# Attention and a maxout network: a pair's rows as seven units, one load each for queries and keys, four loads for values

## The chip, the cores and the metric

The kernel runs on one core of one Trainium2 chip. A core has five engines that run side by side and meet through semaphores: TensorE (PE in the profile; its weight loads are PEld), VectorE (DVE), ScalarE (ACT), GpSimd (POOL) and SyncE (SP), which here does nothing but issue DMA transfers. Transfers run on the core's 16 DMA engines. The metric is the device time of one execution in microseconds; lower is better.

## What is computed

Attention with normed queries and keys, for 8 images (batch entries) and 12 heads of 448 tokens and 64 channels; its output, with the heads side by side as 768 channels, goes through a layer with three weight matrices of which the elementwise largest is kept, and a second layer.

```python
batch, n_heads, seq, head_dim = (8, 12, 448, 64)
n_tokens, d_model, d_ff = (3584, 768, 768)

def rmsnorm(x, g):
    rms = np.sqrt(np.mean(x * x, axis=-1, keepdims=True) + 1e-06)
    return x / rms * g
q_n, k_n = (rmsnorm(q, g_q), rmsnorm(k, g_k))
scores = scale * np.matmul(q_n, k_n.transpose(0, 1, 3, 2))
scores = scores - np.max(scores, axis=-1, keepdims=True)
attn = np.exp(scores)
attn = attn / (np.sum(attn, axis=-1, keepdims=True) + 1e-09)
return np.matmul(attn, v).astype(np.float32)
...
h = np.maximum(np.maximum(x @ w1, x @ w2), x @ w3)
return (h @ w_out).astype(np.float32)
```

All inputs and the output are 32-bit floats.

## The kernel before

**Pairs and units.** The work is cut into 48 pairs of heads (G = 48, six pairs an image, g counts them). A pair has 2 x 448 = 896 rows of queries, of keys and of values, which is seven units of 128 rows: units 0 to 2 are rows of the first head, unit 3 holds the last 64 rows of the first head in the lower 64 partitions and the first 64 of the second head in the upper ones, and units 4 to 6 are rows of the second head. A tile of rows is 128 partitions x 7 units x 64 channels.

**Two ways.** The first six pairs (PLAIN = 6, the first image) are computed in 32-bit floats and turned on PE, because the weights of the network aren't ready yet. From pair 6 on each 32-bit operand is split in two 16-bit parts, a high and a low one, and the products of the parts are added up. Turning (rows to columns) is then done by DMA transposes: keys and queries in line 450 (`turn_rows`), the softmax weights pp into pt in lines 735 and 741 (`turn_weights`, five transposes a pair).

**The exchanged copy of the keys.** The turned keys kt hold the high parts in one half of the partitions and the low parts in the other. `swap_keys` (line 457) makes a second copy with the halves exchanged by two transfers from SBUF to SBUF, and the scores (line 584) are the sum of a matmul with each copy. The first scores of a pair are issued in the last beat of the pair before. `swap_values` (line 558) does the like for the values.

**Loads of rows.** `load_rows` loads queries or keys by four transfers a pair: three units of each head (96 KB, line 342) and 64 rows of each head (16 KB, line 344). Keys are read three neighbouring rows to a partition (runs of 768 bytes in memory), queries one row to a partition (256 bytes). `load_v` loads values by seven transfers (lines 360 to 370) into a tile of four units for each head, so that some rows lie in it twice; most of its rows are read in threes, too. The row order of keys and values is the same, and so doesn't change the result. As three keys of one partition follow each other, the low parts of the softmax weights are written in reversed blocks of 64 (`lower_weights`, line 719), and the values' exchanged copy is met in reversed order. All of these transfers are issued by SyncE, except two of the first pair's keys, which ScalarE issues.

**Order of the work.** The order on every engine is that of the program, written out by hand: `beat(g, i)` with 12 beats a pair. A quarter of a pair (c = i // 3) goes through scores, the row's largest (line 606), exponentials (line 622), division and high part (line 708), low part (line 719) and transposes. Meanwhile `thirds` feeds PE with matmuls of the network for the image before (lines 796 and 856). `later(n, work)` puts work n beats later. SyncE's queue gets in a pair: loads of keys (beat 0) and queries (beat 1) three pairs ahead, the last transposes of weights of the pair before (beat 2), the exchanged values (beat 3), the transposes of keys and queries of the next pair (beats 4 and 5), in beat 5 the values six pairs ahead and the first transpose of weights, in beat 8 the exchanged keys and the second transpose of weights, in beat 11 the third; stores of results and loads of network weights come between. It takes them strictly in this order, and a step that waits holds all that stand behind it.

**Values' largest.** `largest_v` lets DVE look for the largest value of a pair once its values are there, four beats after the load in a pair later on (three in the first pair, which loads the values of seven pairs, one in each of beats 0 to 6); `bound_v` combines six pairs of an image by a small matmul.

**Buffers.** kr and qr have two buffers each, vr seven, pp three, kt, qt and pt two, vs two.

Of the kernel before, what the change touches and what calls it, by code (L numbers as in the profile page):

```python
# [11 lines left out]
F16 = mybir.dt.float16  # L12
AF = mybir.ActivationFunctionType
ALU = mybir.AluOpType
AX = mybir.AxisListType.X

P = 128
# [16 lines left out]


PLAIN = 6


@with_exitstack
def qknorm_attention_maxout_ffn_kernel(  # L40
# [35 lines left out]
    nc = tc.nc  # L76
    B, H, S, D = q.shape
# [35 lines left out]
    def later(beats, work, last=False):  # L113

        due.setdefault(clock[0] + beats, ([], []))[last].append(work)
# [203 lines left out]

    st = {}  # L320

    def at_unit(g, h, c):

        if g < PLAIN:
            return 2 * c + h
        return 4 * h + c

    def rest(g):
        return 6 if g < PLAIN else 3

    def load_rows(g, name, src, on):
        b, pr = divmod(g, NP)
        t = sb.tile([P, UNITS, D], F32, name=name, bufs=2)
        for h, half in enumerate(HALVES):
            rows = src[b, 2 * pr + h]
            first = LEFT * h
            if name == "kr":
                main = rows[first:first + 3 * P].rearrange("(p c) d -> p c d", c=3)
            else:
                main = rows[first:first + 3 * P].rearrange("(c p) d -> p c d", p=P)  # L340
            units = slice(h, 6, 2) if g < PLAIN else slice(4 * h, 4 * h + 3)
            on[h].dma_start(out=t[:, units], in_=main)
            last = rows[0:LEFT] if h else rows[3 * P:S]
            on[h].dma_start(out=t[half, rest(g)], in_=last)
        st.setdefault(g, {})[name] = t

    def load_q(g):
        load_rows(g, "qr", q, (nc.sync, nc.sync))

    def load_k(g):  # L350
        load_rows(g, "kr", k, (nc.sync, nc.sync if g else nc.scalar))


    def load_v(g):
        b, pr = divmod(g, NP)
        t = sb.tile([P, 2, 4, D], F32, name="vr", bufs=7)
        lower, upper = HALVES
        on = nc.sync
        rows = v[b, 2 * pr]
        on.dma_start(  # L360
            out=t[:, 0, 0:3], in_=rows[0:3 * P].rearrange("(p c) d -> p c d", c=3)
        )
        for half in HALVES:
            on.dma_start(out=t[half, 0, 3], in_=rows[3 * P:S])  # L364
        rows = v[b, 2 * pr + 1]
        main = rows[LEFT:S].rearrange("(p c) d -> p c d", c=3)
        on.dma_start(out=t[lower, 1, 0], in_=rows[0:LEFT])
        on.dma_start(out=t[upper, 1, 0:3], in_=main[lower])  # L368
        on.dma_start(out=t[lower, 1, 1:4], in_=main[upper])
        on.dma_start(out=t[upper, 1, 3], in_=main[upper, 2])  # L370
        st.setdefault(g, {})["vr"] = t


# [176 lines left out]
            op=ALU.subtract,  # L550
        )

    def swap_values(g):

        s = st[g]
        s["vs"] = sb.tile([P, 8, D], F16, name="vs", bufs=2)
        for to, of in (HALVES, HALVES[::-1]):
            nc.sync.dma_start(out=s["vs"][to], in_=s["vp"][of, 0])


    SHIFT = (LEFT, 0)
# [135 lines left out]
    def upper_weights(g, c):  # L697
        s = st[g]
        sc, n = s["sc", c], banks(c)
        rs = sb.tile([P, 2], F32, name="rs", bufs=3)  # L700
        nc.vector.tensor_scalar(  # L701
            out=rs[:, :n], in0=sc[:, 1, S + 8:S + 8 + n], scalar1=SUM_EPS,
            scalar2=1.0 / P_UP, op0=ALU.add, op1=ALU.mult,
        )
        nc.vector.reciprocal(rs[:, :n], rs[:, :n])
        pp = sb.tile([P, 2, 2 * S], F16, name="pp", bufs=3)
        for h in range(n):
            nc.scalar.activation(  # L708
                pp[:, h, :S], sc[:, h, :S], AF.Copy, scale=rs[:, h:h + 1]
            )  # L710
        s["pp", c] = pp
        s["rs", c] = rs

    def lower_weights(g, c):

        s = st[g]
        sc, rs, pp = s.pop(("sc", c)), s.pop(("rs", c)), s["pp", c]
        for h in range(banks(c)):
            nc.vector.scalar_tensor_tensor(  # L719
                out=pp[:, h, S:].rearrange("p (u k) -> p u k", k=LEFT)[:, ::-1],  # L720
                in0=sc[:, h, :S].rearrange("p (u k) -> p u k", k=LEFT),
                scalar=rs[:, h:h + 1],
                in1=pp[:, h, :S].rearrange("p (u k) -> p u k", k=LEFT),
                op0=ALU.mult, op1=ALU.subtract,
            )

    def turn_weights(g, c):
        s = st[g]
        pp = s.pop(("pp", c))
        if c == 0:  # L730
            s["pt"] = sb.tile([P, 14, 512], F16, name="pt", bufs=2)
        pt = s["pt"]
        if c < 3:
            first = LEFT + c * P
            nc.sync.dma_start_transpose(  # L735
                out=pt[:, :, first:first + P], in_=pp.rearrange("p h k -> p (h k)")
            )
            return
        for h, half in enumerate(HALVES):
            first = 0 if h else LEFT + 3 * P  # L740
            nc.sync.dma_start_transpose(
                out=pt[:, 7 * h:7 * h + 7, first:first + LEFT], in_=pp[half, 0]
            )


# [1 line left out]
    def add_values(g):  # L747
        s = st[g]
        av = ps_a.tile([P, 512], F32, name="av", tag="a")
        s["av"] = av  # L750
        if g < PLAIN:
            vr, pt = s["vr"], pt_plain(s)
            for u in range(4):
                rows = HALVES[0] if u == 3 else slice(0, P)
                for h, half in enumerate(HALVES):
                    nc.tensor.matmul(
                        av[half, :S], vr[rows, h, u], pt[rows, h, u],
                        start=u == 0, stop=u == 3,
                    )
            return  # L760
        vp, vs, pt = s["vp"], s["vs"], s["pt"]
        steps = [(part, u, u) for u in range(4) for part in range(2)]
        steps += [(2, 2 - i, 4 + i) for i in range(3)]
        for n, (part, u, block) in enumerate(steps):
            for h, half in enumerate(HALVES):
                values = vs[:, 4 * h + u] if part == 2 else vp[:, part, 4 * h + u]
                nc.tensor.matmul(  # L767
                    av[half, :S], values, pt[:, 7 * h + block, SHIFT[h]:SHIFT[h] + S],
                    start=n == 0, stop=n == len(steps) - 1,
                )  # L770
# [228 lines left out]
    def beat(g, i):  # L999
# [44 lines left out]
        if g + 1 < G:  # L1044
# [5 lines left out]
            else:  # L1050
# [3 lines left out]
                    lower_rows(g + 1, "kq"[i - 2])  # L1054
                if i in (4, 5):
                    turn_rows(g + 1, "kq"[i - 4])
                if i == 8:
                    swap_keys(g + 1)

        if n < G:  # L1060
# [9 lines left out]
        if g == 0 and i < 7:  # L1070
            load_v(i)
            later(3, lambda: largest_v(i))
        if 0 < g < G - 6 and i == 5:
            load_v(g + 6)
            later(4, lambda: largest_v(g + 6))
        if g == 0 and i == 9:
            bound_v(0)
        if g > 1 and g % NP == 0 and g < G and i == 1:
# [5 lines left out]
        if PLAIN <= w and i == 0:  # L1084
            lower_v(w)
        if PLAIN <= w and i == 3:
            swap_values(w)

        if g + 3 < G:
            if i == 0:  # L1090
# [54 lines left out]
```

## Time and profile before

| | |
|---|---|
| median of 3 runs | 1278.85 us (1277.87 to 1281.59) |
| the profiled execution: its time | 1279.71 us |
| its span, from first to last instruction | 1277.6 us |
| PE busy | 1054.4 us (83%) |
| DVE busy | 712.9 us (56%) |
| ACT busy | 640.1 us (50%) |
| POOL busy | 615.5 us (48%) |
| mean clock granted to PE | 0.915 of full speed |
| DMA packets of the queue that SyncE feeds | 480736, 166.12 MB, 63.5% of 16 engines' span |

Times in the profile are microseconds, unless marked ns. A group of instructions is shown as line, engine and operation, tile written and tile read, shapes, count; then its busy time in all, the mean of one in ns, and the idle time of the engine just ahead of it with what ended most of that. The timeline shows start, duration and what ran; rows of SPq are SyncE's queue issuing transfers, and their duration is that of issuing, not of the transfer. "Issue to landing" is the transfer's own time. Releasers are inferred from semaphores.

### The profile page before, as it was taken

The page shows a single profiled execution, that of the slowest core. Times are in us where ns is not written, and L with a number is a line of the kernel's source. Part 1 is how long each engine was busy: PE and PEld are TensorE (multiplying, and loading weights), DVE is VectorE, ACT ScalarE, POOL GpSimd, SP SyncE. Part 2 cuts the span into 40 slices and gives each one's busy share as a digit, 9 for nine tenths or more (in the row PEclk, how much of TensorE's full clock was granted, in tenths as well). Part 3 has the DMA queues.
Part 4 walks back from the last instruction along what each step waited for, and adds up shares of the span by engine and source line. Part 5 has one row for each costly group of instructions (what it writes and reads, how often), then busy time and mean ns, then how long its engine had stood idle before and what let it go on. Part 6 is the DMA issues. An engine that isn't in the chain of part 4 may idle for free. (4 is left out here: it accounts for less than half of the span.)

```text
span 1277.6 us, 18009 instructions
## 1 busy us (share of the span) xinstructions
PE 1054.4 (83%) x5850; PEld 545.4 (43%) x5850; DVE 712.9 (56%) x1348; ACT 640.1 (50%) x1437; POOL 615.5 (48%) x661
## 2 busy tenths in 40 slices
PE   5398688779688886887888788788878879999998
PEld 3254344334243443443444344344434435455555
DVE  3499879676455644565455554555545555565110
ACT  3278777456445454553545455354544546564111
POOL 4257968545454553554455455455535545551000
PEclk9598879899798998899889898988988999999999
DMA  4455578777767667776767767676676669885001
GB/s 123 108 155 161 158 166 162 144 132 145 146 124 145 122 134 162 138 129 124 158 132 123 144 137 155 126 142 122 132 155 131 127 128 173 157 142 109 26 1 50
DMA packets 481757, 167.63 MB, mean 131 GB/s; under 512 B 429568, under 2 KB 477440, under 8 KB 481664
## 3 DMA queue, kind: packets, MB, share of 16 engines
q1 hardware_dynamic: 480736, 166.12, 63.5%
q8 instruction: 46, 0.75, 0.3%
q10 hardware_dynamic: 928, 0.38, 0.1%
q14 instruction: 47, 0.39, 0.1%
HBM read 53.54 MB, written 11.01 MB: 51 GB/s over the span
## 5 line engine op out<-in xcount | busy, mean ns | idle before, releaser
L796 PE MATMUL acc<-xt,w_sb 128*128 128x448 f16 x2592 | 550.4, 371 | 0.0
L796 PEld LDWEIGHTS <-w_sb 128*128 128x128 f16 x2592 | 263.3, 103 | 273.8 <-issue 65.2
L622 ACT ACTIVATE sc<-sc,nm 128x448 f32<-128x448 f32 x294 | 178.8, 608 | 238.8 <-DVE nm L606 234.1
L708 ACT ACTIVATE pp<-sc,rs 128x448 f16<-128x448 f32 x294 | 173.0, 634 | 227.8 <-DMA pt<-pp 183.9
L606 DVE TENSOR_REDUCE nm<-sc 128x2 f32<-128x896 f32 x192 | 186.7, 973 | 165.9 <-PE sc L584 94.5
L584 PE MATMUL sc<-kt,qt 128*128 128x448 f16 x504 | 136.8, 386 | 164.9 <-DMA kt<-kt 158.3
L719 DVE SCALAR_TENSOR_TENSOR pp<-sc,rs,pp 128x448 f16<-128x448 f32 x294 | 188.0, 676 | 1.7 <-ACT pp L708 1.7
L856 PE MATMUL acc<-wo_sb,ht 128*128 128x384 f16 x864 | 154.9, 336 | 0.0
L402 POOL TENSOR_TENSOR ri<-ri,half_neg 128x7 f32<-128x7 f32 x96 | 146.4, 1525 | 8.0
L825 POOL COPY hx<-ht 128x128 f16<-128x128 f16 x48 | 15.6, 325 | 271.5 <-DVE ht L820 271.5
L584 PEld LDWEIGHTS <-qt 128*128 128x128 f16 x504 | 48.2, 102 | 222.4 <-DMA kt<-kt 172.7
L548 POOL TENSOR_TENSOR vp<-vr,vp 128x512 f16<-128x512 f32 x42 | 49.2, 1172 | 168.8 <-ACT vp L542 168.8
L856 PEld LDWEIGHTS <-ht 128*128 128x128 f16 x864 | 86.1, 101 | 65.2 <-issue 13.7
L165 DVE TENSOR_REDUCE v_rows<-vr 128x1 f32<-128x512 f32 x48 | 32.8, 684 | 114.9 <-DMA vr<-in_v_dram 114.9
L782 DVE SCALAR_TENSOR_TENSOR xt<-av,xt 128x448 f16<-128x448 f32 x42 | 26.2, 624 | 91.8 <-ACT xt L781 91.7
L767 PE MATMUL av<-pt,vp 128*64 128x448 f16 x672 | 74.0, 360 | 3.5 <-DMA qr<-in_q_dram 1.8
L436 POOL TENSOR_TENSOR kp<-kn,kp 128x448 f16<-128x448 f32 x42 | 45.6, 1085 | 60.9 <-ACT kp L430 60.7
L388 DVE TENSOR_REDUCE ss<-sq 128x7 f32<-128x448 f32 x96 | 57.7, 602 | 13.1 <-ACT sq L379 10.0
L436 POOL TENSOR_TENSOR qp<-qn,qp 128x448 f16<-128x448 f32 x42 | 43.5, 1036 | 26.6 <-ACT qp L430 23.4
L701 DVE TENSOR_SCALAR rs<-sc 128x2 f32<-128x2 f32 (+1 forms) x168 | 26.3, 157 | 52.3 <-ACT sc L622 52.3
L810 DVE TENSOR_TENSOR m<-acc,m 128x448 f32<-128x448 f32 x48 | 29.7, 618 | 42.7 <-PE acc L796 39.4
L767 PEld LDWEIGHTS <-vp 128*64 128x64 f16 x672 | 35.8, 111 | 38.7 <-issue 15.1
(126 smaller groups left out, 1236.7 us busy)
## 6 DMA issues: line engine op xcount, KB each, us to landing
raw<-in_moe_w_dram SPq DMA_DIRECT2D x18, 768.0 KB, 4.5
kt<-kt SPq DMA_DIRECT2D x84, 112.0 KB, 2.9
qr<-in_q_dram SPq DMA_DIRECT2D x96, 96.0 KB, 2.3
out_dram<-osb SPq DMA_DIRECT2D x24, 384.0 KB, 2.8
kr<-in_k_dram SPq DMA_DIRECT2D x95, 96.0 KB, 2.9
vs<-vp SPq DMA_DIRECT2D x84, 64.0 KB, 2.0
vr<-in_v_dram SPq DMA_DIRECT2D x48, 96.0 KB, 2.5
vr<-in_v_dram SPq DMA_DIRECT2D x96, 48.0 KB, 2.2
```

The lines of the kernel that those rows point to most:

```text
L388: nc.vector.tensor_reduce(sums[g % 2][:, KQ[what]], sq, axis=AX, op=ALU.add)
L402: nc.gpsimd.tensor_tensor(out=ri, in0=ri, in1=half_neg[:, at], op=ALU.pow)
L436: nc.gpsimd.tensor_tensor(out=parts[:, :, 1], in0=n, in1=parts[:, :, 0], op=ALU.subtract)
L548: nc.gpsimd.tensor_tensor(out=vp[:, 1], in0=vr.rearrange("p h n d -> p (h n) d"), in1=vp[:, 0], op=ALU.subtract,)
L584: nc.tensor.matmul(sc[:, h, :S], qt[:, 4 * h + c], kt[:, n, keys[h]], start=n == 0, stop=n == 1,)
L606: nc.vector.tensor_reduce(nm[:, :n], sc[:, :n, :S], axis=AX, op=ALU.max, negate=True)
L622: nc.scalar.activation(to, sc[:, h, :S], AF.Exp, bias=nm[:, h:h + 1], accum_out=total,)
L708: nc.scalar.activation(pp[:, h, :S], sc[:, h, :S], AF.Copy, scale=rs[:, h:h + 1])
L719: nc.vector.scalar_tensor_tensor(out=pp[:, h, S:].rearrange("p (u k) -> p u k", k=LEFT)[:, ::-1], in0=sc[:, h, :S].rearrange("p (u k) -> p ...
L767: nc.tensor.matmul(av[half, :S], values, pt[:, 7 * h + block, SHIFT[h]:SHIFT[h] + S], start=n == 0, stop=n == len(steps) - 1,)
L796: nc.tensor.matmul(acc[:, :S], wt[:, wp, c], xs[c][:, xp], start=(c == 0 and n == 0), stop=(c == NCT - 1 and n == 2),)
L856: nc.tensor.matmul(acc[:, :HW], lhs, wo_sb[:, f, wp, half * HW:(half + 1) * HW], start=(f == 0 and n == 0), stop=(f == NFT - 1 and n == 2),)
```

## The change

Tiles of queries, keys and values are all read one row to a partition, in order. Queries and keys of a split pair come in one load of seven units (224 KB) each; for the six plain pairs in three. Values come in four loads: three units of each head, and two for the fourth units of both heads. The names LOADS and the choice of ScalarE as issuer are new: a pair from number 48 on would be loaded by ScalarE, and the pairs are 0 to 47. The low parts of the softmax weights keep their order, and the exchanged copy of the values becomes a shifted copy of three units a head instead of four (`shift_values`, 48 KB instead of 64 KB a transfer). The exchange of the keys is issued in beat 7 instead of 8, the load of values in beat 6 instead of 5, with DVE's search three beats after it instead of four.

```diff
 PLAIN = 6
+LOADS = 48
...
     def load_rows(g, name, src, on):
+
         b, pr = divmod(g, NP)
         t = sb.tile([P, UNITS, D], F32, name=name, bufs=2)
-        for h, half in enumerate(HALVES):
-            rows = src[b, 2 * pr + h]
-            first = LEFT * h
-            if name == "kr":
-                main = rows[first:first + 3 * P].rearrange("(p c) d -> p c d", c=3)
-            else:
-                main = rows[first:first + 3 * P].rearrange("(c p) d -> p c d", p=P)
-            units = slice(h, 6, 2) if g < PLAIN else slice(4 * h, 4 * h + 3)
-            on[h].dma_start(out=t[:, units], in_=main)
-            last = rows[0:LEFT] if h else rows[3 * P:S]
-            on[h].dma_start(out=t[half, rest(g)], in_=last)
+        rows = src[b, 2 * pr:2 * pr + 2].rearrange("h s d -> (h s) d")
+        rows = rows.rearrange("(n p) d -> p n d", p=P)
+        if g < PLAIN:
+            for h in range(2):
+                on[h].dma_start(out=t[:, h:6:2], in_=rows[:, 4 * h:4 * h + 3])
+            on[1].dma_start(out=t[:, 6], in_=rows[:, 3])
+        else:
+            on[0].dma_start(out=t, in_=rows)
         st.setdefault(g, {})[name] = t
 
     def load_q(g):
-        load_rows(g, "qr", q, (nc.sync, nc.sync))
+        load_rows(g, "qr", q, (nc.sync, nc.sync) if g < LOADS else (nc.scalar,))
 
     def load_k(g):
-        load_rows(g, "kr", k, (nc.sync, nc.sync if g else nc.scalar))
+        first = (nc.sync, nc.sync if g else nc.scalar)
+        load_rows(g, "kr", k, first if g < LOADS else (nc.scalar,))
...
         t = sb.tile([P, 2, 4, D], F32, name="vr", bufs=7)
-        lower, upper = HALVES
-        on = nc.sync
-        rows = v[b, 2 * pr]
-        on.dma_start(
-            out=t[:, 0, 0:3], in_=rows[0:3 * P].rearrange("(p c) d -> p c d", c=3)
-        )
-        for half in HALVES:
-            on.dma_start(out=t[half, 0, 3], in_=rows[3 * P:S])
-        rows = v[b, 2 * pr + 1]
-        main = rows[LEFT:S].rearrange("(p c) d -> p c d", c=3)
-        on.dma_start(out=t[lower, 1, 0], in_=rows[0:LEFT])
-        on.dma_start(out=t[upper, 1, 0:3], in_=main[lower])
-        on.dma_start(out=t[lower, 1, 1:4], in_=main[upper])
-        on.dma_start(out=t[upper, 1, 3], in_=main[upper, 2])
+        rows = v[b, 2 * pr:2 * pr + 2]
+        for h in range(2):
+            nc.sync.dma_start(
+                out=t[:, h, 0:3], in_=rows[h, 0:3 * P].rearrange("(u p) d -> p u d", p=P)
+            )
+        for half, part in zip(HALVES, (rows[:, 3 * P:S], rows[:, 0:LEFT])):
+            nc.sync.dma_start(out=t[half, :, 3], in_=part.rearrange("h p d -> p h d"))
...
-    def swap_values(g):
+    def shift_values(g):
...
-        s["vs"] = sb.tile([P, 8, D], F16, name="vs", bufs=2)
-        for to, of in (HALVES, HALVES[::-1]):
-            nc.sync.dma_start(out=s["vs"][to], in_=s["vp"][of, 0])
+        t = s["vs"] = sb.tile([P, 2, 3, D], F16, name="vs", bufs=2)
+        vp = s["vp"][:, 0].rearrange("p (h n) d -> p h n d", h=2)
+        lower, upper = HALVES
+        nc.sync.dma_start(out=t[lower], in_=vp[upper, :, 0:3])
+        nc.sync.dma_start(out=t[upper], in_=vp[lower, :, 1:4])
...
     def lower_weights(g, c):
...
-                out=pp[:, h, S:].rearrange("p (u k) -> p u k", k=LEFT)[:, ::-1],
-                in0=sc[:, h, :S].rearrange("p (u k) -> p u k", k=LEFT),
-                scalar=rs[:, h:h + 1],
-                in1=pp[:, h, :S].rearrange("p (u k) -> p u k", k=LEFT),
-                op0=ALU.mult, op1=ALU.subtract,
+                out=pp[:, h, 1], in0=sc[:, h, :S], scalar=rs[:, h:h + 1],
+                in1=pp[:, h, 0], op0=ALU.mult, op1=ALU.subtract,
...
     def add_values(g):
...
-        steps += [(2, 2 - i, 4 + i) for i in range(3)]
+        steps += [(2, u, 4 + u) for u in range(3)]
...
-                values = vs[:, 4 * h + u] if part == 2 else vp[:, part, 4 * h + u]
+                values = vs[:, h, u] if part == 2 else vp[:, part, 4 * h + u]
...
     def beat(g, i):
...
-                if i == 8:
+                if i == 7:
                     swap_keys(g + 1)
...
-        if 0 < g < G - 6 and i == 5:
+        if 0 < g < G - 6 and i == 6:
             load_v(g + 6)
-            later(4, lambda: largest_v(g + 6))
+            later(3, lambda: largest_v(g + 6))
...
         if PLAIN <= w and i == 3:
-            swap_values(w)
+            shift_values(w)
```

More of the change, by code (lines that the diff above doesn't have):

```diff
@@ L320, in qknorm_attention_maxout_ffn_kernel @@
     st = {}
[L322 to L329, printed above, removed]
     def load_rows(g, name, src, on):
@@ L705, in upper_weights @@
         nc.vector.reciprocal(rs[:, :n], rs[:, :n])
-        pp = sb.tile([P, 2, 2 * S], F16, name="pp", bufs=3)
+        pp = sb.tile([P, 2, 2, S], F16, name="pp", bufs=3)
         for h in range(n):
             nc.scalar.activation(
-                pp[:, h, :S], sc[:, h, :S], AF.Copy, scale=rs[:, h:h + 1]
+                pp[:, h, 0], sc[:, h, :S], AF.Copy, scale=rs[:, h:h + 1]
             )
@@ L735, in turn_weights @@
             nc.sync.dma_start_transpose(
-                out=pt[:, :, first:first + P], in_=pp.rearrange("p h k -> p (h k)")
+                out=pt[:, :, first:first + P], in_=pp.rearrange("p h a k -> p (h a k)")
             )
@@ L741, in turn_weights @@
             nc.sync.dma_start_transpose(
-                out=pt[:, 7 * h:7 * h + 7, first:first + LEFT], in_=pp[half, 0]
+                out=pt[:, 7 * h:7 * h + 7, first:first + LEFT],
+                in_=pp[half, 0].rearrange("p a k -> p (a k)"),
             )
```

## The prediction

> **What bounds the kernel now.** I read the page's costliest groups first, because PE is the busiest engine. The matmuls of the scores carry nearly all of its waiting, and one transfer ends it, the exchanged copy of the turned keys (issued in line 457):
>
> ```profile
> span 1277.6 us, 18009 instructions
> ...
> L584 PE MATMUL sc<-kt,qt 128*128 128x448 f16 x504 | 136.8, 386 | 164.9 <-DMA kt<-kt 158.3
> ...
> kt<-kt SPq DMA_DIRECT2D x84, 112.0 KB, 2.9
> ```
>
> The last column of the second row says that PE stood 164.9 us ahead of these matmuls, 158.3 of it for that copy. The third row (the page's DMA issues) says that one copy needs 2.9 us from issue to landing, so it is not slow: it is issued late. So the next view is the timeline of SyncE's queue (start, duration, line), here one whole pair of heads, from one exchange to the next:
>
> ```profile
> 1026.20 1.77 SPq L457 DMA_DIRECT2D kt<-kt  x2
> 1028.09 3.82 SPq L735 DMA_TRANSPOSE pt<-pp  x2
> 1032.03 0.98 SPq L342 DMA_DIRECT2D kr<-in_k_dram  x1
> 1033.06 0.51 SPq L344 DMA_DIRECT2D kr<-in_k_dram  x1
> ...
> 1037.24 0.67 SPq L344 DMA_DIRECT2D qr<-in_q_dram  x1
> 1038.02 2.53 SPq L741 DMA_TRANSPOSE pt<-pp  x2
> 1040.66 1.17 SPq L558 DMA_DIRECT2D vs<-vp  x2
> 1041.93 1.24 SPq L450 DMA_TRANSPOSE kt<-kp  x1
> 1043.27 1.24 SPq L450 DMA_TRANSPOSE qt<-qp  x1
> 1044.57 0.57 SPq L360 DMA_DIRECT2D vr<-in_v_dram  x1
> ...
> 1048.30 0.59 SPq L370 DMA_DIRECT2D vr<-in_v_dram  x1
> 1048.99 1.55 SPq L735 DMA_TRANSPOSE pt<-pp  x1
> 1050.59 1.77 SPq L457 DMA_DIRECT2D kt<-kt  x2
> ```
>
> Each row starts within about 0.1 us of the end of the one before. SyncE issues without pause, 24.39 us a pair (1050.59 - 1026.20), and nothing else in the kernel needs that long. **SyncE's issuing is the bound.** The same view where no loads are left, two and three pairs from the end:
>
> ```profile
> 1113.07 1.90 SPq L457 DMA_DIRECT2D kt<-kt  x2
> 1115.09 3.82 SPq L735 DMA_TRANSPOSE pt<-pp  x2
> 1120.29 2.67 SPq L741 DMA_TRANSPOSE pt<-pp  x2
> 1123.08 2.25 SPq L558 DMA_DIRECT2D vs<-vp  x2
> 1125.43 1.24 SPq L450 DMA_TRANSPOSE kt<-kp  x1
> 1126.77 1.25 SPq L450 DMA_TRANSPOSE qt<-qp  x1
> 1128.11 1.62 SPq L735 DMA_TRANSPOSE pt<-pp  x1
> 1129.83 1.72 SPq L457 DMA_DIRECT2D kt<-kt  x2
> 1131.65 3.62 SPq L735 DMA_TRANSPOSE pt<-pp  x2
> 1138.51 2.50 SPq L741 DMA_TRANSPOSE pt<-pp  x2
> ```
>
> Now SyncE has gaps, and the chain that ended last runs through PE alone there:
>
> ```profile
> 1112.93 0.38 PE sc L591 x4
> ...
> 1131.51 0.38 PE sc L591 x4
> ...
> 1135.97 0.76 PE sc L584 x4
> ...
> 1150.09 0.38 PE sc L591 x4
> ```
>
> Equal points of three pairs are 18.58 us apart (1131.51 - 1112.93, 1150.09 - 1131.51). That is PE's own pair, with softmax and splitting at their full pace beside it. So the trace holds a sample of the kernel with SyncE unburdened: 18.58 against 24.39.
>
> The last view sets both stretches side by side (window and length; busy time of PE, its loads, DVE, ACT, POOL with counts; granted clock; DMA share; GB/s):
>
> ```profile
> 1028.09:1052.47 24.38, 20.21 (x116) 10.43 (x116) 14.17 (x29) 11.92 (x28) 13.61 (x16) 0.93 0.67 131
> 1115.09:1131.65 16.56, 16.56 (x102) 8.53 (x99) 11.83 (x25) 11.34 (x26) 9.71 (x12) 1.00 0.79 148
> ```
>
> DVE, ACT and POOL need at most 14.2 us a pair, so none of them is next. The 16 DMA engines are busy 0.67 x 24.38 = 16.3 us a pair with loads and 0.79 x 16.56 = 13.1 without: the loads cost them about 3.2 us.
>
> **The change part by part.** Where do the sums apply? The first exchange of the even stretch is quoted below; the one at 1113.07 is 38 pairs later, 933.52 us, so 24.57 a pair with the stores of results that some pairs carry (24.39 without). After 1113.07 come 164.5 us that hold no loads of rows and only work that the change leaves as it is.
>
> ```profile
> 179.55 1.13 SPq L457 DMA_DIRECT2D kt<-kt  x2
> ```
>
> *Queries and keys.* Eight issues a pair become two. The eight take 5.99 us (1032.03 to 1038.02). What does a load of 896 pieces cost to issue? No row shows one. The nearest is a weight block, 768 KB in 768 pieces:
>
> ```profile
> 10.41 1.17 SPq L218 DMA_DIRECT2D raw<-in_moe_w_dram  x2
> 11.72 0.58 SPq L342 DMA_DIRECT2D kr<-in_k_dram  x1
> ```
>
> Two of these take 1.17 and the load behind them 0.58, like any other, so issue does not grow with the pieces: 0.55 each, the lower end. The upper end is 1.24, the row of a transpose that reads a tile of the same 128 x 7 units. I take 0.55, as it is a plain load. The first behind the transposes keeps its 0.98. So 0.98 + 0.55 and two gaps of 0.05 make 1.63: 4.36 saved. Eight rows that nothing stretched (0.98 and seven of about 0.6 with gaps) would take 5.1, and 3.5 would be saved. The upper end gives back up to 1.4.
>
> *Values.* Seven issues take 4.42 us (1044.57 to 1048.99), 0.63 each with gaps; four take 2.53: 1.89 saved. Together 5.4 to 6.25 a pair leave SyncE 18.3 to 19.2 of the 24.57; I take 18.8. SyncE was the issuer of these loads before, too (the branch for ScalarE needs a pair 48, and the last is 47), so that part of the change moves nothing.
>
> *Exchange in beat 7, values in beat 6.* The load of values goes behind the first transpose of weights, the exchange stays behind both. What is issued between the transposes of keys and queries and the exchange is then 1.62 + 2.53 in place of 4.42 + 1.55: only the 1.9 that is counted already. The beat itself matters once SyncE has slack. Does the copy then come in time? Put the four loads into the quoted pair without loads, behind 1128.11: the exchange ends at 1129.83 + 1.72 + 2.53 = 1134.1; its second half, issued some 0.85 sooner, lands 2.9 later, at 1136.1. PE wants it at 1135.97. That is 0.2 late; with the usual 1.17 for vs in place of 2.25 it is 0.9 early. DVE's search for the largest value stays in its beat (one later, one less of delay), and its wait for the loads shrinks with them.
>
> *Where SyncE's next turn falls.* In the same pair the transposes from 1131.65 now end at 1137.8, the two loads at 1139.4, and the next step is due at 1138.51: 0.9 late, or 0.2 early with vs at 1.17. Stores come on top: three an image and two more every second image, so 27 in the seven images of these 38 pairs; at 0.6, an issue like any other, 0.4 a pair. So SyncE (18.8) and PE (18.58) are nearly even and hand each other a wait now and then. I take **19.0 us a pair**, 0.2 over the larger.
>
> *Splitting and shifted copy.* DVE's low parts lose their reversed blocks; DVE is hidden (14.17 of 24.38), and if it became bound this could only help: 0. The shifted values are 48 KB a copy in place of 64, still two issues: 0. The matmuls are as many.
>
> *More and smaller pieces.* Keys were 384 pieces a pair, queries 896, values 512; now 896, 896 and 1024. So 1792 become 2816 for nearly the same bytes. The engines' 3.2 us stay 3.2 (by bytes) or become 5.0 (by pieces); with 13.1 and about 1.1 for stores (some 245 KB a pair, at the rate of the loads' 752 KB in 3.2) that is 17.4 to 19.2 a pair. By the upper end it would equal my pair; I keep it as a bound. The Trainium skill speaks against this part: "DMA: Bandwidth & Descriptors", section "Why small descriptors are slow (HBM only)", gives a 256-byte piece 11 cycles for 8 of data. By that a 768-byte run cut in three costs 33 cycles for 27, and the estimate for the loads would be at most 3.9 us, inside my ends. No run here shows a piece's price by itself.
>
> *Start.* The first beats load seven pairs' values, and PE waits for the largest value of the first six:
>
> ```profile
> 48.74 0.48 SPq L370 DMA_DIRECT2D vr<-in_v_dram  x1
> ...
> 52.80 0.56 PE L517 MATMUL most<-v_most,ones_c 128*128 128x1 f32 x2 [13.67 <-DVE v_most L510]
> ...
> 160.13 1.30 PE L584 MATMUL sc<-kt,qt 128*128 128x448 f16 x3 [6.73 <-DMA kt<-kt]
> ```
>
> The first row is the last load of the sixth pair. Ahead of it 18 issues of values go (0.64 each with gaps, 11.5) and 8 of keys and queries (0.6, 4.8): some 16 us sooner. The 13.67 us wait of the second row goes, with what other chains keep: I take 13, between 8 and 17. At the first split pair (third row) seven loads become four ahead of the exchange: 3 of the 6.73.
>
> *Sum.* 179.55 - 13 - 3 = 163.5; 38 x 19.0 = 722; 164.5 for the end; 2.1 around the span (the profiled execution took 1279.71 us for a span of 1277.6). 163.5 + 722 + 164.5 + 2.1 = **1052 us**. The profiled execution is 0.9 above the median of 1278.85, which changes nothing.
>
> **The rivals.**
>
> *PE alone is the bound.* SyncE's savings hold at their larger end and its waits fit into its slack: 18.1 to 18.58 a pair (some pairs hold a little less work of the network than the quoted ones), 1018 to 1036 us. For it: the pairs without loads. Against it: stores, and the exchange that is just in time.
>
> *Transfers or dearer issue give part of it back.* At 1.24 for a large load the pair is 20.4; if the loads' service doubled to 6.4, the engines need 13.1 + 6.4 + 1.1 = 20.6, with transposes blocking SyncE meanwhile: 330.1 + 38 x 20.5 = 1109 us. For it: 17.4 to 19.2 of 19.0 leaves the engines little air, and two transposes in a row take 3.82 (1028.09) where one takes 1.55, so the queue holds SyncE up already. Against it: the share is 0.67 now. The skill's same page, in "Specifications", gives 512 B as the least size for full rate, which points this way.
>
> *Slower than before.* The place is the DMA queue from loads to transposes: if small pieces hold the engines for more than 24.57 - 13.1 - 1.1 = 10.4 us a pair, transposes land too late and the pair grows beyond today's. That is 10.4 x 16 / 2816 = 59 ns for a piece on one engine, against 3.2 x 16 / 1792 = 29 ns now, where half of the pieces already have 256 B. At 65 ns the pair is 25.6: 330.1 + 973 = 1303 us.
>
> *It does not do what it says.* The issue time saved comes back whole as longer transposes, because the queue behind SyncE was the limit: 1263 us, the 16 at the start aside. Against it: DMA at 0.67, and load rows of even 0.5 to 0.6 us.
>
> **How the numbers follow.** Forecast, 18.6 to 19.6 a pair (1037 to 1075 us): 0.52. PE alone: 0.20. Part given back (1075 to 1170): 0.24. Nothing gained: 0.02. Slower: 0.02. The range leaves out about one in ten on each side: 1020 to 1112, which takes in both ends of the issue price and of the start. A measurement of this kernel tells 0.3% (4 us) from no change: faster 0.97, same 0.01, slower 0.02.
>
> **What would show it.** PE's wait for kt falls from 158 to under 30 us; exchanges stand 18.6 to 19.6 us apart; two rows of about 0.55 to 1.0 for keys and queries and four of 0.6 for values; PE's granted clock near 1.00 in the pairs, DMA share about 0.9 (17.4 of 19.0); no wait of 13 us near 40. Wrong if large loads take over 1.2 us to issue, if the transposes behind them grow by more than a microsecond, or if another wait (weights for pt, values for DVE) takes the place of kt.

## The result and the profile after

The changed kernel takes 1091.12 us (median of 4 runs, 1090.79 to 1095.35); the kernel before took 1278.36 us beside it. The ratio is 0.854, 95% interval 0.8513 to 0.8566. The forecast was 1052 us and the range 1020 to 1112. The profiled execution took 1095.35 us, the longest of the four, with a span of 1093.6.

The page of the changed kernel, with the rows that answer to those of before (busy times; the scores' matmuls with PE's wait ahead of them; the exchanged copy and its time to land):

```profile
PE 996.9 (91%) x5850; PEld 526.8 (48%) x5850; DVE 705.5 (65%) x1348; ACT 637.6 (58%) x1437; POOL 615.2 (56%) x661
...
L573 PE MATMUL sc<-kt,qt 128*128 128x448 f16 x504 | 123.6, 360 | 54.6 <-DMA kt<-kt 41.7
...
kt<-kt SPq DMA_DIRECT2D x84, 112.0 KB, 2.3
```

PE's wait for the exchanged keys fell from 158.3 to 41.7 us. The same matmuls also became cheaper, 360 ns in place of 386. That is the granted clock, as the windows by stage show, first of the kernel before, then of the changed one. The two stages are the first nine pairs after the exchange of pair 7 and the 29 behind them (the cut in the first fence is some 7 us off the exchange of pair 16). The columns are window and length, busy time of PE, its loads, DVE, ACT and POOL with counts, granted clock, DMA share, GB/s:

```profile
179.55:400.00 220.45, 176.79 (x954) 87.76 (x954) 146.63 (x280) 124.83 (x274) 125.07 (x130) 0.89 0.74 145
400.00:1113.07 713.07, 596.30 (x3322) 299.99 (x3320) 386.12 (x778) 353.89 (x823) 365.29 (x412) 0.92 0.71 139
```

```profile
164.32:357.22 192.90, 171.94 (x994) 86.39 (x995) 146.94 (x284) 126.44 (x278) 130.35 (x135) 0.96 0.86 169
357.22:927.82 570.60, 542.59 (x3269) 282.50 (x3269) 379.94 (x772) 348.95 (x814) 357.19 (x404) 1.00 0.90 170
```

Over both stages PE was idle for 160.4 us before (933.5 - 773.1) and 49.0 after (763.5 - 714.5), and its busy time fell by 58.6 us for nearly the same matmuls. The granted clock accounts for that fall: its mean over both stages is 0.913 before and 0.990 after, and 773.1 x 0.913 / 0.990 = 713, against 714.5 measured. So of the 170 us that these 38 pairs lost, 111 were waiting and 59 were slower clock. The rest of the gain is the start: the exchange of pair 7 came at 179.55 and comes at 164.32. The wait of 13.67 us for the values' largest stands at 6.87 now:

```profile
39.71 0.56 PE L504 MATMUL most<-v_most,ones_c 128*128 128x1 f32 x2 [6.87 <-DVE v_most L497]
```

What follows the exchange of pair 45 takes 165.8 us, as before (164.5).

These exchanges in SyncE's timeline, of pairs 7, 16 and 45, give the pace:

```profile
164.32 1.14 SPq L444 DMA_DIRECT2D kt<-kt  x2
...
357.22 1.19 SPq L444 DMA_DIRECT2D kt<-kt  x2
...
927.82 1.71 SPq L444 DMA_DIRECT2D kt<-kt  x2
```

That is 20.09 us a pair over all 38, against 24.57 before and 19.0 in the forecast: 21.43 in the first nine and 19.68 in the other 29.

One later pair in SyncE's queue, in the same form as the pair that the prediction shows:

```profile
834.25 1.15 SPq L444 DMA_DIRECT2D kt<-kt  x2
835.51 4.87 SPq L720 DMA_TRANSPOSE pt<-pp  x2
840.47 1.00 SPq L336 DMA_DIRECT2D kr<-in_k_dram  x1
841.58 0.56 SPq L336 DMA_DIRECT2D qr<-in_q_dram  x1
842.24 2.50 SPq L726 DMA_TRANSPOSE pt<-pp  x2
844.83 0.65 SPq L546 DMA_DIRECT2D vs<-vp  x1
845.54 0.62 SPq L547 DMA_DIRECT2D vs<-vp  x1
846.26 1.25 SPq L437 DMA_TRANSPOSE kt<-kp  x1
847.61 1.24 SPq L437 DMA_TRANSPOSE qt<-qp  x1
848.94 1.58 SPq L720 DMA_TRANSPOSE pt<-pp  x1
850.58 1.70 SPq L353 DMA_DIRECT2D vr<-in_v_dram  x2
852.32 1.32 SPq L357 DMA_DIRECT2D vr<-in_v_dram  x2
853.74 1.19 SPq L444 DMA_DIRECT2D kt<-kt  x2
```

There are still hardly any gaps: 19.49 us of nearly pure issuing. SyncE is the bound of the later pairs after the change, too (e4 and e9 below test it). Adding up all rows of its queue between the exchanges of pairs 16 and 41, 25 pairs that have all loads, gives these means (us a pair; each group is the sum of its rows' durations, "between" the sum of the pauses from one row to the next):

```
                        before  after  e6     e3     e5     e4     e9
loads of keys, queries   4.79   1.46   5.02   1.48   1.33   -      -
loads of values          4.38   3.00   4.66   2.63   2.97   3.11   -
transposes of weights    8.12   8.61   8.19   8.40   8.33   8.40   9.41
transposes of keys, q.   2.61   2.60   2.59   2.54   2.54   2.57   2.56
exchange of keys         1.64   1.22   1.66   1.67   1.23   1.23   1.40
copy of values           1.22   1.37   1.30   1.28   1.32   1.32   1.29
stores                   0.43   0.42   0.40   0.47   0.41   0.53   0.42
between                  1.58   1.18   1.16   1.16   1.25   1.93   3.52
pair                    24.78  19.86  24.99  19.64  19.40  19.09  18.60
```

(e6, e3, e5, e4 and e9 are experiments below.)

### The profile page after: what moved, and what is told of

It is laid out like the page before. It is cut to its first block, busy times and chain, and to the rows that moved or that the text cites. A ratio compares the mean times of both kernels' runs of the same rounds, so it can differ in the third digit from the quotient of the medians.

```text
span 1093.6 us, 17471 instructions
## 1 busy us (share of the span) xinstructions
PE 996.9 (91%) x5850; PEld 526.8 (48%) x5850; DVE 705.5 (65%) x1348; ACT 637.6 (58%) x1437; POOL 615.2 (56%) x661
## 3 DMA queue, kind: packets, MB, share of 16 engines
q1 hardware_dynamic: 525600, 164.70, 75.4%
## 5 line engine op out<-in xcount | busy, mean ns | idle before, releaser
L782 PE MATMUL acc<-xt,w_sb 128*128 128x448 f16 x2592 | 517.3, 355 | 0.0
L782 PEld LDWEIGHTS <-w_sb 128*128 128x128 f16 x2592 | 252.7, 98 | 245.9 <-issue 18.0
L573 PE MATMUL sc<-kt,qt 128*128 128x448 f16 x504 | 123.6, 360 | 54.6 <-DMA kt<-kt 41.7
L842 PE MATMUL acc<-wo_sb,ht 128*128 128x384 f16 x864 | 148.5, 326 | 0.7 <-DVE ht L806 0.5
L842 PEld LDWEIGHTS <-ht 128*128 128x128 f16 x864 | 83.2, 98 | 61.1 <-issue 4.7
L753 PE MATMUL av<-pt,vp 128*64 128x448 f16 x672 | 71.6, 356 | 0.0
L753 PEld LDWEIGHTS <-vp 128*64 128x64 f16 x672 | 34.5, 109 | 34.1 <-issue 12.5
```

The costliest lines, as they stand in the source:

```text
L573: nc.tensor.matmul(sc[:, h, :S], qt[:, 4 * h + c], kt[:, n, keys[h]], start=n == 0, stop=n == 1,)
L753: nc.tensor.matmul(av[half, :S], values, pt[:, 7 * h + block, SHIFT[h]:SHIFT[h] + S], start=n == 0, stop=n == len(steps) - 1,)
L782: nc.tensor.matmul(acc[:, :S], wt[:, wp, c], xs[c][:, xp], start=(c == 0 and n == 0), stop=(c == NCT - 1 and n == 2),)
L842: nc.tensor.matmul(acc[:, :HW], lhs, wo_sb[:, f, wp, half * HW:(half + 1) * HW], start=(f == 0 and n == 0), stop=(f == NFT - 1 and n == 2),)
```

## The experiments

Theory A: SyncE's queue set the pace before and still does in the later pairs, and what a part is worth is what its issues take there. Theory B: the small pieces load the DMA engines, which then hold SyncE up. Theory C: the gain comes from the exchange's earlier place in the order. Edits are against the changed kernel, unless told otherwise. "Pair" is the mean distance of exchanges over the 38 pairs.

| run | median, us | ratio to before, interval | pair | exchange of pair 7 at |
|---|---|---|---|---|
| before (beside the changed kernel) | 1278.36 | | 24.57 | 179.55 |
| changed | 1091.12 | 0.8513 to 0.8566 | 20.09 | 164.32 |
| e1_kq_four | 1208.52 | 0.9419 to 0.9473 | 23.12 | 163.50 |
| e2_v_seven | 1172.72 | 0.9141 to 0.9184 | 21.65 | 181.12 |
| e3_order_before | 1085.72 | 0.8461 to 0.8501 | 19.92 | 159.32 |
| e4_kq_on_act | 1068.69 | 0.8330 to 0.8372 | 19.36 | 162.94 |
| e5_long_runs | 1078.89 | 0.8402 to 0.8441 | 19.61 | 162.00 |
| e6_all_three_back | 1290.13 | 1.0053 to 1.0095 | 24.80 | 180.30 |
| e7_values_last | 1087.84 | 0.8460 to 0.8507 | 20.00 | 162.48 |
| e8_order_and_act | 1066.15 | 0.8295 to 0.8342 | 19.32 | 164.08 |
| e9_all_on_act | 1057.57 | 0.8238 to 0.8301 | 19.15 | 162.23 |
| e10_even | 1063.08 | 0.8290 to 0.8346 | 19.27 | 160.17 |
| e11_less_decoding | 1062.06 | 0.8283 to 0.8333 | 19.23 | 161.85 |
| e12_act_even | 1056.79 | 0.8241 to 0.8288 | 19.08 | 162.68 |

### Undoing one part at a time

Queries and keys in four loads:

```diff
-            on[0].dma_start(out=t, in_=rows)
+            for to, n in (
+                (slice(0, P), slice(0, 3)), (HALVES[0], 3),
+                (slice(0, P), slice(4, 7)), (HALVES[1], 3),
+            ):
+                on[0].dma_start(out=t[to, n], in_=rows[to, n])
```

> Queries and keys of a split pair in four loads each again, in the new row order; the rest as changed. Theory A (the number of issues in SyncE's queue sets the pace): six more issues at 0.55 to 0.65 us, 3.3 to 4.0 us a pair, 38 pairs: 1215 to 1245 us, exchanges 23 to 24 us apart. Rival C (the gain comes from the exchange's place in the order, not from fewer issues): under 1150 us.

Measured: 1208.52 us, 117 more than the changed kernel; 3.0 us a pair. That is 6 us under A's range and far from C: the exchange stands in its new beat and the time is lost all the same. In the 25 pairs of the table the loads of keys and queries take 5.03 us of SyncE instead of 1.46, and a pair 23.08 instead of 19.86. PE's list of waits shows where the time goes:

```profile
PE sc L577 <- DMA kt<-kt: 112.9, 37, 6.7
```

112.9 us in 37 waits, against 41.7 in the changed kernel. So six issues a pair of 16 and 96 KB, dropped from the queue, carry the larger part of the gain.

Values in seven loads of the old sizes:

```diff
-        for h in range(2):
-            nc.sync.dma_start(
-                out=t[:, h, 0:3], in_=rows[h, 0:3 * P].rearrange("(u p) d -> p u d", p=P)
-            )
-        for half, part in zip(HALVES, (rows[:, 3 * P:S], rows[:, 0:LEFT])):
-            nc.sync.dma_start(out=t[half, :, 3], in_=part.rearrange("h p d -> p h d"))
+        main = [rows[h, 0:3 * P].rearrange("(u p) d -> p u d", p=P) for h in range(2)]
+        nc.sync.dma_start(out=t[:, 0, 0:3], in_=main[0])
+        for half in HALVES:
+            nc.sync.dma_start(out=t[half, 1, 0:3], in_=main[1][half])
+        for half, first in zip(HALVES, (3 * P, 0)):
+            for h in range(2):
+                nc.sync.dma_start(out=t[half, h, 3], in_=rows[h, first:first + LEFT])
```

> Values in seven loads of the old sizes again, in the new row order. Theory A: three more issues, 1.6 to 1.9 us a pair over some 36 pairs, 58 to 70 us, and 5 to 9 us at the start, where PE waits for the values' largest: 1150 to 1175 us. Rival C: under 1110 us.

Measured: 1172.72 us, 82 more, in A's range, with 1.56 us a pair (59 us over 38 pairs), at its lower end. The start is off: the exchange of pair 7 comes 16.8 us later, not 5 to 9. It stands at 181.12, about where it stood before, though the plain pairs keep their three loads of keys and queries. So the gain at the start needs the merged loads of values.

The old order, with merged loads:

```diff
-                if i == 7:
+                if i == 8:
                     swap_keys(g + 1)
...
-        if 0 < g < G - 6 and i == 6:
+        if 0 < g < G - 6 and i == 5:
             load_v(g + 6)
-            later(3, lambda: largest_v(g + 6))
+            later(4, lambda: largest_v(g + 6))
```

> Exchange back in beat 8 and load of values back in beat 5, DVE's search four beats after it; loads merged as changed. Theory A: the issues are the same and their sum sets the pace: 1088 to 1100 us. Rival C: most of the gain is lost, over 1130 us.

Measured: 1085.72 us, below the expected 1088 and 5 below the changed kernel; the intervals of the ratios do not touch. C falls. The new order doesn't help, it costs half a per cent. The table of SyncE's queue shows one effect of the order: right behind a transpose of weights the loads of values take 3.00 us instead of 2.63, and right behind it the exchange takes 1.67 instead of 1.22. These two cancel. With the old order a pair takes 19.64 instead of 19.86, and the row that is shorter by that much is the transposes of weights (8.40 instead of 8.61). Why they are shorter is not shown.

All three undone (the edits of e1, e2 and e3 together):

> Loads of queries and keys in four, of values in seven, exchange and values in their old beats: what is left of the change are the row order, the low parts without reversed blocks and the shifted copy. Theory A: these bring nothing, 1270 to 1290 us. If the three parts add up by themselves (117 for queries and keys, 82 for values, -5 for the order over the changed kernel's 1091) it is about 1285. A clear rest (under 1260) would be the reversed blocks' or the shifted copy's.

Measured: 1290.13 us, 9.8 over the kernel before that ran beside it (ratio 1.0053 to 1.0095): as the sum of the parts says (1285), or a little more. So the loads' number is all of the gain, and what remains of the change (row order, low parts without reversed blocks, shifted copy) costs about 10 us. In SyncE's queue it is the loads that take longer than before (5.02 instead of 4.79 us for keys and queries, 4.66 instead of 4.38 for values), partly at the cost of the pauses (1.16 instead of 1.58); the transposes of weights hardly do (8.19 instead of 8.12).

### Small pieces

```diff
-            on[0].dma_start(out=t, in_=rows)
+            rows = src[b, 2 * pr:2 * pr + 2].rearrange("h s d -> (h s) d")
+            on[0].dma_start(out=t, in_=rows.rearrange("(p n) d -> p n d", p=P))
...
-                out=t[:, h, 0:3], in_=rows[h, 0:3 * P].rearrange("(u p) d -> p u d", p=P)
+                out=t[:, h, 0:3], in_=rows[h, 0:3 * P].rearrange("(p u) d -> p u d", p=P)
```

> The changed kernel with the same loads, but each partition reads neighbouring rows: seven for queries and keys (1792 bytes in a run), three for values (768 bytes), so 768 pieces a pair in place of 2816. The rows come in another order, so that heads are mixed and the output is another. Theory B (small pieces load the DMA engines, which hold SyncE up in transposes and in the loads of values): transposes of weights fall from 8.67 us a pair to the 8.1 of before, loads of values from 0.75 to 0.6 each, 1.0 to 1.2 us a pair: 1045 to 1058 us. Theory A (the number of issues alone): 1085 to 1096 us.

Measured: 1078.89 us, 12 less: between the two ranges and in neither. The same bytes come in fewer packets (the page's row of SyncE's DMA queue: packets, bytes, share of 16 engines), first the changed kernel, then this one:

```profile
q1 hardware_dynamic: 525600, 164.70, 75.4%
```

```profile
q1 hardware_dynamic: 436512, 164.70, 73.1%
```

In SyncE's queue the transposes of weights take 8.33 instead of 8.61 us, the loads of keys and queries 1.33 instead of 1.46, and a pair takes 0.46 less. So pieces have a price, less than half of what B expected: the loads of values didn't get cheaper (2.97). This run has 768 pieces a pair, fewer than the 1792 of before, so its 12 us are the price of 2048 pieces a pair, not of the 1024 that the change added. On the change's own row order only e6 speaks: some 10 us, with the low parts and the shifted copy in it. From the page of the Trainium skill that the prediction weighed ("DMA: Bandwidth & Descriptors", section "Why small descriptors are slow (HBM only)"), it had an estimate of at most 0.7 us more engine time a pair. The pages' DMA rows agree with that bound: the share of 16 engines' span was 63.5% of 1277.6 us before and is 75.4% of 1093.6, 13 us more in all, 0.3 a pair.

### Taking load off SyncE

Queries and keys of split pairs issued by ScalarE:

```diff
-LOADS = 48
+LOADS = 6
```

> The changed kernel, but ScalarE issues the loads of queries and keys of the split pairs (LOADS = 6). Theory A: SyncE loses 1.46 us and two gaps a pair, and PE (18.3 to 18.6 a pair) takes over from 19.8: 1040 to 1060 us. Theory B (the 16 DMA engines, 0.90 busy, hold SyncE up, so that it doesn't matter who issues): 1083 to 1098 us. If ScalarE's issuing gets in the way of its exponentials, slower than 1098.

Measured: 1068.69 us, 22 less, outside both ranges: not B, as the same transfers from another issuer save time, but A's range began at 31 less. SyncE has pauses now (1.93 instead of 1.18 us a pair), and the later 29 pairs come to 18.93 us. The first nine stay at 20.75.

With the old order on top (the edits of e3 and e4 together):

> Queries and keys of split pairs loaded by ScalarE, with the old order (exchange in beat 8, values in beat 5). If the two gains add up (22 and 5 us): 1060 to 1066 us. If PE's own work is the floor by now: 1066 to 1070 us, like the kernel with ScalarE's loads alone.

Measured: 1066.15 us. That is on the border of the two ranges. Two and a half microseconds less than e4 is hardly clear of the spread (e4's runs 1067.87 to 1070.55, here 1061.89 to 1067.42; the intervals of the ratios overlap), so whether the five of the old order add up is open. The windows of this run show how little room there is:

```profile
164.08:351.75 187.67, 169.61 (x983) 85.20 (x981) 145.66 (x282) 126.75 (x278) 128.69 (x134) 0.96 0.90 172
351.75:898.06 546.31, 538.55 (x3268) 284.05 (x3267) 380.44 (x773) 348.95 (x813) 358.22 (x404) 1.00 0.97 178
```

From pair 16 on PE is busy for 538.55 of 546.31 us at full clock: there PE is nearly the bound, with 7.8 us of waiting left. In the nine pairs before it is not.

The values of pairs 13 to 47 issued by ScalarE as well (on the kernel of e8):

```diff
         rows = v[b, 2 * pr:2 * pr + 2]
+        on = nc.scalar if g >= 2 * PLAIN + 1 else nc.sync
         for h in range(2):
-            nc.sync.dma_start(
+            on.dma_start(
...
-            nc.sync.dma_start(out=t[half, :, 3], in_=part.rearrange("h p d -> p h d"))
+            on.dma_start(out=t[half, :, 3], in_=part.rearrange("h p d -> p h d"))
```

> As the kernel with the old order and ScalarE's loads of queries and keys (1066 us); ScalarE issues the values of pairs 13 to 47, too. If SyncE still holds PE up: 1050 to 1060 us. If PE is the floor from pair 16 on (98.6% busy there at full clock): 1062 to 1070 us; more than 1070 if four more issues a pair delay ScalarE's exponentials.

Measured: 1057.57 us, in the first of the ranges: SyncE still held PE up a little in e8. The later 29 pairs take 18.61 us each; the prediction read PE's own pair as 18.58. PE's list of waits (of the whole run) and the window of the first 28 of these pairs:

```profile
PE sc L574 <- DVE pp L708: 13.9, 9, 3.1
...
PE sc L574 <- DMA kt<-kt: 7.8, 3, 6.1
...
350.20:872.99 522.79, 522.09 (x3189) 276.89 (x3187) 368.39 (x751) 339.80 (x795) 350.25 (x395) 1.00 1.00 181
```

PE is busy for 522.09 of 522.79 us, and the DMA share in the last columns is 1.00 without holding PE up.

Values behind the exchange (order alone, loads on SyncE):

```diff
-        if 0 < g < G - 6 and i == 6:
+        if 0 < g < G - 6 and i == 8:
             load_v(g + 6)
```

> The changed kernel with the load of values two beats later, so that it stands behind the exchange of the keys. The sum of issues is the same. Theory A: the exchange comes 2.5 us earlier against the transposes, but the sum of 19.7 us a pair stays, and so does the time: 1082 to 1096 us, with PE's wait moved to another tile. Rival C (what is left of PE's wait is only the exchange's place): the 42 us of kt go, 1050 to 1065 us.

Measured: 1087.84 us, as A said. PE's wait moves to another tile, as expected:

```profile
PE sc L573 <- DVE pp L707: 28.3, 22, 3.7
PE sc L573 <- DMA kt<-kt: 18.2, 8, 6.2
...
DVE v_rows L168 <- DMA vr<-in_v_dram: 115.2, 39, 6.5
```

The exchange no longer comes late as often (18.2 us in place of 41.7), but PE now waits for the low parts of the weights (28.3 us in place of 12.5). The last line fits that: DVE, which writes the low parts, now waits 115.2 us for the values that it searches, in place of 60.0. The wait moved with the load that went to the back, and the sum of issues kept the time.

### The first nine split pairs

Two of three decoding steps of the output weights left out (on the kernel of e8):

```diff
-        for stage in range(3):
+        for stage in range(3 if kind == "in" else 1):
             later(2 + stage, lambda stage=stage: decode(raw, f, stage), True)
```

> As the kernel with the old order and ScalarE's loads of queries and keys (1066 us); two of three decoding steps of the output weights are left out, so that these weights and the output are others. They are 12 operations of about 1.2 us on DVE in the first split pairs, 14 us. If DVE's decoding of weights makes these nine pairs long (20.9 us against 18.8 later): 5 to 12 us less, 1054 to 1061 us, the nine at 20.3 or under. If not: 1063 to 1069.

Measured: 1062.06 us, 4 less: between the two ranges and in neither, and the runs overlap with e8's (1061.37 to 1062.71 against 1061.89 to 1067.42). The nine pairs went from 20.85 to 20.59 us, 2.3 us in all, with 11.3 us less of DVE's busy time in them (134.36 instead of 145.66). So this decoding is at most a small part of what makes them long.

Network units spread evenly (on the kernel of e8):

```diff
-        thirds(THIRDS[i] + (len(queue) > 1 and i % 6 == 4))
+        thirds(THIRDS[i])
```

> As the kernel with the old order and ScalarE's loads of queries and keys (1066 us); the extra network units that a pair gets while two images wait are left out of the order. If pairs of uneven length on PE cost time (short ones wait for SyncE, long ones for PE): 5 to 15 us less, 1051 to 1061. If not: 1062 to 1075, as the units left over then stand behind the last pair.

Measured: 1063.08 us, 3 less: within the runs' spread (1061.51 to 1065.43 against 1061.89 to 1067.42), and in the range of "if not". No gain is shown. The edits of e9 and e10 together:

> The two edits that still brought something, put together: ScalarE issues queries, keys and values of the later pairs, the old order, and no extra network units for a pair while two images wait. With ScalarE's loads PE is busy from pair 16 on (18.6 a pair), so that uneven pairs can no longer cost anything there: 1053 to 1060 us, within 4 us of the kernel without the last edit (1057.6). If the two gains add up in full (8.5 and 3 us below 1066): 1054.

Measured: 1056.79 us (1054.27 to 1058.89), in the first range and not to be told from e9's 1057.57. Both e9 and e12 beat the changed kernel by 3%.

## Why the prediction was right, and where its size was off

**The bound: right.** SyncE's issuing set the pace. Putting issues back loses what they take (e1, e2, e6), moving them to ScalarE gains more (e4, e9), changing their order gains nothing (e3, e7). The time came out inside the range of 1020 to 1112, but not in the forecast's own stretch (1037 to 1075, chance 0.52): 1091 lies in that of the rival "part given back" (1075 to 1170, chance 0.24). Of the signs, the granted clock, the DMA share and the two cheap loads of keys and queries came; PE's wait for kt stayed at 41.7 us (forecast: under 30) and the exchanges stand 20.09 us apart (18.6 to 19.6).

**The start and the end: right in size, the start in part by luck.** The sum had 163.5 us to the exchange of pair 7 and 164.5 behind that of pair 45; measured are 164.3 and 165.8. The last load of the sixth pair's values is issued by 36.21 us, 13 us sooner (16 in the prediction), and the matmul behind it starts 13.1 us sooner, as the sum had it, though half of its wait is left (6.87 of 13.67 us). The 3 us at the first split pair did not come: that wait for the exchanged keys is 6.07 us in place of 6.73. In its place 3.9 us more came up to the exchange of pair 6 (137.62 in place of 154.64), and from there to that of pair 7 it took 1.8 longer than before; why, no run shows.

**The pair: too short.** The sum had 38 x 19.0 = 722 us, the trace of the profiled execution (1095.35 us) has 763.5. This is nearly the whole miss (41.5 us, beside 1.3 in the tail and 0.8 in the start), and it has two halves:

- *The later 29 pairs*, 0.68 too short each, 20 us. The step at fault is "SyncE 18.8". In the 25 pairs of the table it was 19.86. The eight loads of keys and queries were sized from one pair in which they took 5.99 us with pauses; the mean was 4.79, or some 5.3 with them, so less was saved. Four loads of values take 3.00, not about 2.3 without pauses, as they stand right behind a transpose (2.63 in e3, where they don't). The transposes of weights grew by 0.49. Small pieces are part of it at most: with them and the old loads the transposes took 8.19 (e6) against 8.12 before, and 2048 fewer of them took 0.28 off (e5). The rest is open. The exchange got 0.42 cheaper, which the sum had not counted and which happens to pay for most of that. The rival "part given back" was this mechanism at a smaller size: the issue price stayed near its lower end (1.46 for both loads), and the transposes gave back half a microsecond, where the rival's pair was 1.7 over 18.8.
- *The first nine*, 2.4 too short each, 22 us. The step at fault is "DVE, ACT and POOL need at most 14.2 us a pair, so none of them is next". It was read from one later pair. In the first ones the network's weights are still being decoded and split. These are the windows of the first two of the nine, and of the third and the seventh:

```profile
164.32:186.06 21.74, 19.78 (x116) 9.79 (x116) 18.91 (x40) 19.62 (x40) 18.55 (x17) 1.00 0.96 214
186.06:210.13 24.07, 22.53 (x132) 10.98 (x129) 21.61 (x37) 17.34 (x37) 21.18 (x20) 1.00 0.86 165
210.13:231.08 20.95, 16.17 (x80) 7.59 (x80) 15.33 (x29) 10.60 (x25) 12.63 (x15) 0.84 0.89 186
...
296.65:315.84 19.19, 15.86 (x74) 7.51 (x76) 10.31 (x21) 9.68 (x23) 9.71 (x11) 0.76 0.98 182
```

In the first two DVE's 18.91 and 21.61 us, ACT's 19.62, POOL's 18.55 and 21.18 leave no room for a pair of 19.0. Before, pairs of more than 26 us covered it. That is 7.8 of the 22 us. In the other seven no single engine is that full in every pair; there PE waits, and in the pairs with one long wait of about 5 us (the last two rows) its granted clock is lower as well, 0.84 and 0.76. PE's timeline in two later ones of the nine, and its waits over all nine:

```profile
263.00 0.93 PE L573 MATMUL sc<-kt,qt 128*128 128x448 f16 x4 [2.22 <-DVE pp L707]
269.46 0.93 PE L573 MATMUL sc<-kt,qt 128*128 128x448 f16 x4 [2.12 <-DVE pp L707]
...
299.98 1.30 PE L573 MATMUL sc<-kt,qt 128*128 128x448 f16 x3 [5.40 <-DMA kt<-kt]
```

```profile
PE sc L573 <- DMA kt<-kt: 10.5, 3, 5.4
PE sc L573 <- DVE pp L707: 9.0, 6, 2.6
PE sc L580 <- DVE pp L707: 1.8, 3, 1.1
```

Half of the waiting is for late exchanges, half for the softmax's low parts. With SyncE relieved the nine go from 21.43 to 20.6 to 20.9 us and stay there (e4, e8, e9, e11), so about a third of their 2.4 us at most is SyncE's. Which of the engines' work sets the rest is not settled: decoding the output weights is about a tenth of it (e11), and leaving out the splitting of the weights was not tried.

**Side effects.** That the exchange would be "just in time" was right in place: PE waited for it 24 times, 1.7 us in the mean (41.7 / 24). The term of nothing for the low parts and the shifted copy is not told apart from the row order in e6, whose 10 us hold all three. The engines' time for the loads stayed near its lower end: 0.3 us more a pair over the whole span, where the prediction had 0 to 1.8. The 752 KB of loads a pair that it counts are 704 by their sizes; its 1.1 us for stores stand by that. The 0.2 for mutual waits was not tested by itself.

**The rivals.** PE alone as the bound (1018 to 1036 us) did not come about with loads on SyncE; e9 shows the state it described from pair 16 on. Slower by small pieces: their price is real but half a microsecond a pair for 2048 of them (e5), far from the 5.6 that it needed. "It does not do what it says" fell: the rows of the loads got 4.71 us shorter a pair (9.17 to 4.46), and the transposes of weights gave 0.49 of it back.

## What to carry to other kernels

Where one queue issues all transfers, add up its rows between two equal points of the loop. If there are no pauses, issuing may be the bound, and moving a few loads to an engine with time to spare tests it. Here it was, and the number of issues counted far more than their pieces (117 and 82 us in e1 and e2, 12 in e5). Take such a sum over many rounds of the loop, not over one, and read the hidden engines in every stage that the sum covers, the first rounds above all: what a slow bound covers there comes to light when it goes. An order in which something comes "sooner" was worth nothing while the queue as a whole was full (e3, e7).

## What was not expected of the hardware

The forecast took the issue of a plain load as hardly dependent on its size, and that held: 0.56 us for 224 KB in 896 pieces where nothing stretched it, about 0.5 for 16 KB, while a transpose took 1.25 to 2.4. Not expected was that what stands right behind a transpose of weights takes longer to issue: loads of values 3.00 instead of 2.63 us for four, the exchange 1.67 instead of 1.22 for two. And a DMA share of 1.00 over 523 us (e9) stood beside a PE that was busy for 99.9% of it: the share alone did not make the transfers the bound.
